# A score bank for the second FFN group of a double step, normalizations deferred by length, and casts moved ahead of their PE transposes

## The chip, the cores and the metric

The kernel runs on one core of a Trainium2 chip. The metric is the device time of one execution in microseconds (us). The time before is 454.0 us, the median of two runs (453.2 to 454.79).

## The reference, cut to what matters

```python
B, H, S, Nb, D = (8, 8, 576, 16, 64)
k_all = concatenate([beacon_k, k]);  v_all = concatenate([beacon_v, v])
scores = (q @ k_all.T) / sqrt(D)         # causal over k; the 16 beacon keys are always seen
a = exp(scores - max);  a /= a.sum(-1) + 1e-9
x = (a @ v_all), transposed to (4608, 512)           # 4608 = 8 * 576 rows
out = (relu(x @ w_gate) * (x @ w_val)) @ w_out       # 512 -> 1536 -> 512
```

All matmuls take bf16 (so says every record of one in the traces) and write tiles of FP32; the PE transposes write bf16 ones. The kernel takes no maximum away before the exponential; it checks at the end that the row sums were in a safe range, and has a general path for when they were not.

## The kernel before

The attention of one pair of heads is cut into four steps, by chunks of queries: step 0 fills a chunk of 240 columns, steps 1 and 2 together one of 256, step 3 one of 80. Two steps make a double step of the loop. In a double step PE makes two score groups, two groups of the FFN (an "up" group is four matmuls for g and four for u, a "down" group twelve), and the value products of the double step before. ScalarE (ACT) takes exponentials and relu, VectorE (DVE) takes reciprocals and products, GpSimd (Pool) masks and casts.

A bank is here what a tile of 512 FP32 columns takes in PSUM. The pool of scores has two tiles of two banks, the pool of value products two of one bank, and the FFN pool two of one bank: 2x2 + 2 + 2, eight banks in all.

```python
    s_ps = ...tile_pool(name="s_ps", bufs=2, space=PSUM)    # tiles [P, 2, 512] FP32: two banks each
    o_ps = ...tile_pool(name="o_ps", bufs=2, space=PSUM)    # [P, 2, 256]: product and row sums
    f_ps = ...tile_pool(name="f_ps", bufs=2, space=PSUM)    # [P, 512]: g, u, down
    ...
    def normalize(pr, i):                     # only if i ends its chunk
        nc.vector.reciprocal(r, o[:, 1, :cn])
        nc.vector.tensor_mul(xT[:, pr.p, t0:t0 + cn], o[:, 0, :cn], r)

        def up(self, nf, c0, c1):
            g = f_ps.tile([P, M_TILE], FP32, name="f")
            ... 4 matmuls into g
            nc.scalar.activation(gs[:, :n], g[:, :n], AF.Relu)
            u = f_ps.tile([P, M_TILE], FP32, name="f")
            ... 4 matmuls into u
            nc.vector.tensor_mul(self.h[:, nf, c0:c1], gs[:, :n], u[:, :n])

        def turn_pair(b, x, p, copy, ps_pool):
            h = half.tile([P, 4, P], BF16, name="half")
            copy(h..., wide[b, x, p]...)                        # cast to bf16
            ps = ps_pool.tile([P, 4, P], BF16, ...)
            for r in range(4):
                nc.tensor.transpose(ps[:, r], h[:, r], ident)   # PE, at once after its cast
            copy(dst..., ps...)

        for s0 in range(0, len(work) + STRIDE, STRIDE):         # STRIDE = 2: a double step
            ...
            for s in now:
                ... qk, and the first softmax
            for s in now:
                ... later actions, the second softmax
                if queue:
                    queue.pop(0)()                              # one FFN group
                if waiting:
                    normalize(*waiting.pop())
            for s in range(s0 - STRIDE, s0):
                ... av(pairs[b, p], i)
                waiting.append((pairs[b, p], i))
                if s == s0 - STRIDE or not queue:
                    normalize(*waiting.pop())
        ...
        for j, g in enumerate(queue):                           # FFN groups left after the attention
            if j == 2:
                ok = rows_in_range()
            if j == 8:
                in_range = count(ok)
            g()
```

So the first normalization of a double step is done at once, and the second waits until the first FFN group of the next double step has been issued. Of the first batches (0 and 1), a pair's steps run in the order 0, (1, 2), 3. From batch 2 on, a batch does (1, 2) for its four pairs and then (0, 3) for its four pairs.

Of the kernel before, what the change touches and what calls it, by code (L numbers as in the profile page):

```python
# [10 lines left out]
FP32 = mybir.dt.float32  # L11
BF16 = mybir.dt.bfloat16
# [134 lines left out]
def kernel(  # L147
# [12 lines left out]
    nc = tc.nc  # L160
    B, H, S, D = q.shape
    Nb = beacon_k.shape[2]
    P = 128
    d_model = H * D
    n_tokens = B * S
    d_ff = moe_w_gate.shape[1]
    KM, NF = d_model // P, d_ff // P
    NP = H // 2
# [3 lines left out]
    M_TILE = 512  # L172
# [4 lines left out]
    ident = const.tile([P, P], BF16, name="ident")  # L177
# [10 lines left out]
    main = ctx.enter_context(ExitStack())  # L188
    kvq = main.enter_context(tc.tile_pool(name="kvq", bufs=2))
    stage = main.enter_context(tc.tile_pool(name="stage", bufs=11))  # L190
    half = main.enter_context(tc.tile_pool(name="half", bufs=6))
    psb = main.enter_context(tc.tile_pool(name="psb", bufs=4))
    nrm = main.enter_context(tc.tile_pool(name="nrm", bufs=2))
    fsb = main.enter_context(tc.tile_pool(name="fsb", bufs=2))
# [1 line left out]
    s_ps = main.enter_context(tc.tile_pool(name="s_ps", bufs=2, space=bass.MemoryType.PSUM))  # L196
    o_ps = main.enter_context(tc.tile_pool(name="o_ps", bufs=2, space=bass.MemoryType.PSUM))
    f_ps = main.enter_context(tc.tile_pool(name="f_ps", bufs=2, space=bass.MemoryType.PSUM))
# [101 lines left out]
    def normalize(pr, i):  # L300
        ci = CHUNK_OF_STEP[i]
        cq0, cn, _, last = CHUNKS[ci]
        if i != last:
            return
        o, batch = pr.o[ci], pr.batch
        r = batch.r[:, pr.p, cq0:cq0 + cn]
        nc.vector.reciprocal(r, o[:, 1, :cn])  # L307
        t0 = batch.b * S + cq0
        nc.vector.tensor_mul(xT[:, pr.p, t0:t0 + cn], o[:, 0, :cn], r)  # L309
        batch.chunks += 1  # L310
        if batch.chunks == NP * len(CHUNKS):
            nc.sync.dma_start(
                rsum[2 * batch.b:2 * batch.b + 2],
                batch.r.rearrange("(a x) p s -> a x (p s)", a=2)[:, 0])


    class Ffn:
# [1 line left out]
        def __init__(self, m0):  # L319
            self.m0, self.h = m0, None  # L320

        def up(self, nf, c0, c1):
            n = c1 - c0
            if self.h is None:
                self.h = fsb.tile([P, NF, M_TILE], BF16, name="hT")
            x = xT[:, :, self.m0 + c0:self.m0 + c1]
            g = f_ps.tile([P, M_TILE], FP32, name="f")
            for ki in range(KM):
                nc.tensor.matmul(g[:, :n], wg[:, ki, nf * P:(nf + 1) * P], x[:, ki],  # L329
                                 start=(ki == 0), stop=(ki == KM - 1))  # L330
            gs = fsb.tile([P, M_TILE], FP32, name="g")
            nc.scalar.activation(gs[:, :n], g[:, :n], AF.Relu)  # L332
            u = f_ps.tile([P, M_TILE], FP32, name="f")
            for ki in range(KM):
                nc.tensor.matmul(u[:, :n], wv[:, ki, nf * P:(nf + 1) * P], x[:, ki],  # L335
                                 start=(ki == 0), stop=(ki == KM - 1))
            nc.vector.tensor_mul(self.h[:, nf, c0:c1], gs[:, :n], u[:, :n])  # L337
# [9 lines left out]
            nc.sync.dma_start(out[m:m + P, :], ob)  # L347

        def groups(self, c0, c1, d0, d1):
            return ([lambda nf=nf: self.up(nf, c0, c1) for nf in range(NF)]  # L350
                    + [lambda ms=ms: self.down(ms) for ms in range(d0, d1)])

    def rows_in_range():

# [23 lines left out]
    with tc.manual_schedule():  # L378
# [3 lines left out]
        rest = S - WIDE  # L382
        wide = {}
        vec, act, pool = nc.vector.tensor_copy, nc.scalar.copy, nc.gpsimd.tensor_copy
# [13 lines left out]
                nc.sync.dma_start(t[p0:p0 + a.shape[1]].rearrange("p (h d) -> p h d", d=D),  # L398
                                  a.rearrange("h p d -> p h d"))

        def turn_pair(b, x, p, copy, ps_pool):
            h = half.tile([P, 4, P], BF16, name="half")
            copy(h.rearrange("x r (h d) -> x h r d", d=D),  # L403
                 wide[b, x, p].rearrange("x (h r d) -> x h r d", h=2, d=D))
            ps = ps_pool.tile([P, 4, P], BF16, name="f" if ps_pool is f_ps else "s")
            for r in range(4):
                nc.tensor.transpose(ps[:, r], h[:, r], ident)  # L407
            dst, off = (batches[b].kT, Nb) if x == "k" else (batches[b].qT, 0)
            copy(dst[:, p, off:off + WIDE].rearrange("x (p r) -> x p r", r=4),  # L409
                 ps.rearrange("x r p -> x p r"))  # L410

        def turn_tail(b, x, copy, ps_pool):
            n = rest + (Nb if x == "k" else 0)
            h = half.tile([P, d_model], BF16, name="half")
            copy(h[:n], wide[b, x][:n])  # L415
            ps = ps_pool.tile([P, NP, P], BF16, name="f" if ps_pool is f_ps else "s")
            for p in range(NP):
                nc.tensor.transpose(ps[:, p, :n], h[:n, p * P:(p + 1) * P], ident[:n, :n])
            if x == "k":
                copy(batches[b].kT[:, :, Nb + WIDE:Stot], ps[:, :, :rest])  # L420
                copy(batches[b].kT[:, :, :Nb], ps[:, :, rest:n])
            else:
                copy(batches[b].qT[:, :, WIDE:], ps[:, :, :rest])
# [18 lines left out]
        ahead, later = {}, {}  # L442

        def at(step, action, when=later):
            when.setdefault(step, []).append(action)

        for p in range(NP):
            at(p, lambda p=p: turn_pair(0, "k", p, vec, f_ps), ahead)
            at(p, lambda p=p: turn_pair(0, "q", p, act, f_ps), ahead)
            if p == 0:  # L450
                at(p, lambda: turn_tail(0, "k", vec, f_ps), ahead)
        at(4, lambda: turn_tail(0, "q", vec, f_ps), ahead)
        for t, step in enumerate((0, 1, 2, 4, 4)):
            at(step, lambda t=t: batches[0].cast("v", t, pool))
        for w, step in zip(weights, (0, 0, 1, 1, 2, 2, 4, 4, 4)):
# [4 lines left out]
        def fetch_wide(b, load, turn):  # L460
            at(load, lambda: batches.append(Batch(b)))
            units = [lambda p=p, x=x: load_pair(b, x, p) for p in range(NP) for x in "kq"]
            units[2:2] = [lambda: load_tail(b, "k")]
            units[5:5] = [lambda: batches[b].load("v", 0), lambda: batches[b].load("v", 1)]
            units += [lambda: load_tail(b, "q")]
            units += [lambda t=t: batches[b].load("v", t) for t in range(2, NKT)]
            for j, u in enumerate(units):
                at(load + j * 2 // 3, u)
            for p in range(NP):
                at(turn + p, lambda p=p: turn_pair(b, "k", p, vec, s_ps))  # L470
                at(turn + p, lambda p=p: turn_pair(b, "q", p, act, s_ps))
            at(turn + 1, lambda: turn_tail(b, "k", vec, s_ps))
            at(turn + 4, lambda: turn_tail(b, "q", vec, s_ps))
            for t in range(NKT):
                at(turn + t, lambda t=t: batches[b].cast("v", t, pool))

# [14 lines left out]
        for b in range(B):  # L491
# [7 lines left out]
                ready[len(work)] = (b + 1) * S  # L499
            if b == 0:  # L500
                work += [None] * GAP
        fetch_wide(1, 4, 17)
        for b in range(2, B):
            fetch(b, 16 * (b - 1) + GAP)

# [3 lines left out]
        queue, have, pairs, waiting = [], 0, {}, []  # L509
        STRIDE = 2  # L510
# [7 lines left out]
        for s0 in range(0, len(work) + STRIDE, STRIDE):  # L518
            have = ready.get(s0 - STRIDE, have)
            while spans and spans[0][1] <= have:  # L520
                add_ffn()
            now = [s for s in range(s0, s0 + STRIDE) if s < len(work)]
            for s in now:
                for action in ahead.get(s, []):
                    action()
                if work[s]:
                    b, p, i = work[s]
                    qk(pairs.setdefault((b, p), Pair(batches[b], p)), i)
                    if s == s0 or s < 4:
                        softmax(pairs[b, p], i)  # L530
            for s in now:
                for action in later.pop(s, []):
                    action()
                if work[s] and not (s == s0 or s < 4):
                    b, p, i = work[s]
                    softmax(pairs[b, p], i)
                if queue:
                    queue.pop(0)()
                if waiting:
                    normalize(*waiting.pop())  # L540
            for s in range(s0 - STRIDE, s0):
                if 0 <= s < len(work) and work[s]:
                    b, p, i = work[s]
                    av(pairs[b, p], i)

                    waiting.append((pairs[b, p], i))
                    if s == s0 - STRIDE or not queue:
                        normalize(*waiting.pop())
        for w in waiting:
            normalize(*w)  # L550
        while spans:
# [1 line left out]
        for j, g in enumerate(queue):  # L553
            if j == 2:
                ok = rows_in_range()
            if j == 8:
                in_range = count(ok)
            g()
    main.close()
    with tc.If(in_range < 2 * B):  # L560
        general_path(tc, q, k, v, beacon_k, beacon_v, out, ident, wg, wv, wo)
# [30 lines left out]
```

## Time and profile before

| what | before |
|---|---|
| time | 454.0 us |
| span of the profiled execution, granted clock | 447.7 us, 0.989 |
| PE busy | 401.4 us, 90% |
| period of one batch in the steady part (start of a block of down groups to the next) | 44.1 us |
| first scores of batch 1 | 69.65 us |

The first fence is from the page of the kernel before: its busy line, and two lines of the span in 40 slices (busy tenths of PE, and the granted clock in tenths).

```profile
PE 401.4 (90%) x3681; PEld 218.2 (49%) x3681; DVE 249.5 (56%) x355; ACT 200.5 (45%) x313; POOL 123.3 (28%) x283
...
PE   2479579898988999999999999999999788999995
...
PEclk9999989999999999999999999999999989999998
```

PE is busy 90% of the span, but that number says little here. The records of PE overlap: the record of the u group at 241.93 us lasts 1.03 us, and that of the next g begins 0.86 us after its start. What can be trusted is the distance from the first start of a group to the first start of the next. A group of four 512-column matmuls that has nothing in its way takes 0.86 us, and one of 48 such matmuls takes 10.36 us, 215.8 ns each.

The next fence is the wait list of the kernel before: engine, tile and line that waited, what for, us in total, number of times, longest.

```profile
PE o L294 <- DVE xT L309: 12.0, 11, 2.3
...
PE f L418 <- DVE half L415: 5.4, 2, 3.9
...
PE s L407 <- DVE half L403: 4.0, 3, 1.7
```

L294 is the value product, L309 the product that ends a normalization, L403 and L415 are casts, L407 and L418 are PE transposes. The timeline shows single places (start, duration, engine, line, operation, out<-in, idle time before and what ended it):

```profile
50.53 0.62 PE L407 MATMUL s<-ident,half 128*128 128x128 bf16 x8 [1.75 <-DVE half L403]
...
54.13 0.62 PE L407 MATMUL s<-ident,half 128*128 128x128 bf16 x8 [1.31 <-DVE half L403]
...
242.79 1.03 PE L329 MATMUL f<-xT,wg 128*128 128x512 bf16 x4
...
243.06 0.69 DVE L337 TENSOR_TENSOR hT<-g,f 128x512 bf16<-128x512 f32 x1 [6.83 <-PE f L335]
...
243.80 1.02 PE L335 MATMUL f<-xT,wv 128*128 128x512 bf16 x4
...
253.74 1.75 DVE L307 RECIPROCAL r<-o 128x256 f32<-128x256 f32 x1
...
255.53 0.42 DVE L309 TENSOR_TENSOR xT<-o,r 128x256 bf16<-128x256 f32 x1
...
256.00 0.23 PE L294 MATMUL o<-e,v 128*64 128x80 bf16 x2 [0.67 <-DVE xT L309]
```

Three losses are in it. At 50.53 and 54.13 us PE waits for a cast that was issued just in front of the transposes that read it. At 242.79 the second g of a double step takes until 243.80, 1.01 us rather than 0.86: the u behind it needs the bank of the first u, and DVE's product reads that bank until 243.06 + 0.69 = 243.75. The wait list doesn't show this loss, because the record of g, which lasts until 242.79 + 1.03 = 243.82, counts as busy until then. And at 256.00 a value product waits for a bank that a deferred 256-column reciprocal (1.75 us) and product still hold.

### The profile page before, as it was taken

The numbers are of one execution on the slowest core, as the hardware profiler recorded it, in microseconds if no ns is written. First come the engines' busy times: TensorE is split into PE (matmuls) and PEld (weight loads), VectorE is DVE, ScalarE is ACT, GpSimd is POOL, SyncE is SP. The second block draws the span as 40 slices with busy tenths as digits, with TensorE's granted clock in tenths as the row PEclk, the third lists the DMA queues.
The fourth block names the chain that finished last, engine by engine and source line by source line (L and its number), as shares of the span: only waits on it lengthen the run. The fifth ranks groups of instructions, "written<-read, shape, count | busy, mean of one in ns | idle before, by whom it ended". The sixth has DMA issues, their size and how long they took to land.

```text
span 447.7 us, 9258 instructions
## 1 busy us (share of the span) xinstructions
PE 401.4 (90%) x3681; PEld 218.2 (49%) x3681; DVE 249.5 (56%) x355; ACT 200.5 (45%) x313; POOL 123.3 (28%) x283
## 2 busy tenths in 40 slices
PE   2479579898988999999999999999999788999995
PEld 1257446466567445554555455545554343444442
DVE  3457745747579368537853785378637863331320
ACT  3446336356455545454544554446455312322321
POOL 1842204342454444224422442243112100000000
PEclk9999989999999999999999999999999989999998
DMA  9999945885995783379447863790110002002002
GB/s 221 226 211 227 186 102 101 163 152 107 156 202 125 179 184 78 85 197 171 92 91 192 157 116 83 160 180 15 49 48 2 1 4 92 2 0 95 0 16 85
DMA packets 143522, 51.00 MB, mean 114 GB/s; under 512 B 129120, under 2 KB 138848, under 8 KB 143456
## 3 DMA queue, kind: packets, MB, share of 16 engines
q1 hardware_dynamic: 137152, 45.09, 48.6%
q0 software_dynamic: 5776, 4.72, 6.6%
q8 instruction: 31, 0.51, 0.5%
q10 hardware_dynamic: 544, 0.52, 0.3%
q14 instruction: 19, 0.16, 0.1%
HBM read 38.27 MB, written 9.44 MB: 107 GB/s over the span
## 4 chain that ended last, share of the span: by engine, by line
PE 79%; DVE 12%; issue 4%; ACT 2%; DMA 1%; SPq 0%; ACTq 0%; DVEq 0%
PE f L342 21%; PE f L335 20%; PE f L329 19%; PE o L294 11%; DVE r L307 7%; PE s L263 6%; DVE hT L337 3%; DVE xT L309 1%; DMA raw<-in_beacon_k_dram 1%; ACT g L332 1%; ACT half L403 1%; PE s L407 0%; PE f L407 0%; ACT qT L409 0%; DVE half L415 0%
## 5 line engine op out<-in xcount | busy, mean ns | idle before, releaser
L337 DVE TENSOR_TENSOR hT<-g,f 128x512 bf16<-128x512 f32 (+4 forms) x132 | 77.5, 587 | 141.5 <-PE f L335 118.4
L271 ACT ACTIVATE e<-s 128x736 bf16<-128x736 f32 (+3 forms) x128 | 110.5, 864 | 95.4 <-PE s L263 94.9
L307 DVE RECIPROCAL r<-o 128x240 f32<-128x240 f32 (+2 forms) x96 | 129.7, 1351 | 21.9 <-PE o L294 21.9
L329 PE MATMUL f<-xT,wg 128*128 128x512 bf16 (+4 forms) x528 | 117.0, 344 | 6.1 <-ACT g L332 2.7
L274 POOL TENSOR_SCALAR_AFFINE_SELECT e<-e 128x256 bf16<-128x256 bf16 (+2 forms) x160 | 58.8, 387 | 221.0 <-ACT e L271 211.2
L335 PE MATMUL f<-xT,wv 128*128 128x512 bf16 (+4 forms) x528 | 114.9, 340 | 0.6
L332 ACT ACTIVATE g<-f 128x512 f32<-128x512 f32 (+4 forms) x132 | 68.6, 520 | 67.3 <-PE f L329 65.5
L342 PE MATMUL f<-wo,hT 128*128 128x512 bf16 x432 | 97.3, 383 | 0.3 <-ACT g L332 0.3
L335 PEld LDWEIGHTS <-wv 128*128 128x128 bf16 x528 | 51.0, 97 | 55.5 <-issue 18.7
L329 PEld LDWEIGHTS <-wg 128*128 128x128 bf16 x528 | 47.0, 98 | 48.2 <-issue 11.9
L294 PE MATMUL o<-e,v 128*64 128x80 bf16 (+4 forms) x704 | 58.5, 239 | 12.0 <-DVE xT L309 12.0
L342 PEld LDWEIGHTS <-hT 128*128 128x128 bf16 x432 | 41.7, 99 | 51.1 <-issue 4.0
L294 PE MATMUL o<-e,ones 128*64 128x80 bf16 (+4 forms) x704 | 53.4, 233 | 0.0
L294 PEld LDWEIGHTS <-v 128*64 128x64 bf16 (+1 forms) x704 | 35.3, 112 | 36.0 <-issue 26.3
L345 ACT COPY ob<-f 128x512 f32<-128x512 f32 x36 | 21.1, 585 | 68.1 <-PE f L342 62.7
L263 PE MATMUL s<-qT,kT 64*128 64x80 bf16 (+3 forms) x704 | 36.1, 233 | 2.5 <-ACT qT L409 2.0
L309 DVE TENSOR_TENSOR xT<-o,r 128x240 bf16<-128x240 f32 (+2 forms) x96 | 34.3, 358 | 3.3
L294 PEld LDWEIGHTS <-ones 128*64 128x64 bf16 (+1 forms) x704 | 35.4, 113 | 0.1
L239 POOL CAST half<-raw 128x512 bf16<-128x512 f32 (+2 forms) x60 | 35.0, 611 | 0.0
L263 PEld LDWEIGHTS <-kT 64*128 64x128 bf16 x704 | 22.4, 96 | 9.1 <-issue 3.1
L239 POOL CAST v<-raw 128x512 bf16<-128x512 f32 (+1 forms) x40 | 24.4, 616 | 8.0 <-DMA raw<-in_v_dram 8.0
L407 PEld LDWEIGHTS <-half 128*128 128x128 bf16 x64 | 4.6, 114 | 15.1 <-DVE half L403 9.7
(36 smaller groups left out, 50.1 us busy)
## 6 DMA issues: line engine op xcount, KB each, us to landing
out_dram<-ob SPq DMA_DIRECT2D x36, 256.0 KB, 2.2
raw<-in_q_dram SPq DMA_DIRECT2D x30, 256.0 KB, 4.2
raw<-in_k_dram SPq DMA_DIRECT2D x26, 256.0 KB, 5.0
raw<-in_v_dram SPq DMA_DIRECT2D x24, 256.0 KB, 3.8
raw<-in_v_dram SPq DMA_DIRECT2D x8, 224.0 KB, 4.1
wg<-in_moe_w_gate_dram POOLq DMA_DIRECT2D x4, 384.0 KB, 12.0
wv<-in_moe_w_val_dram POOLq DMA_DIRECT2D x4, 384.0 KB, 14.4
wo<-in_moe_w_out_dram POOLq DMA_DIRECT2D x1, 1536.0 KB, 28.3
```

The lines of the kernel that those rows point to most:

```text
L239: copy(dst, self.raw[x, t][:n])
L263: nc.tensor.matmul(s[:, a, c:c + n], pr.batch.kT[rows, pr.p, kt * P:(kt + 1) * P], pr.batch.qT[rows, pr.p, q0:q0 + n], start=True, stop=True)
L271: nc.scalar.activation(e[:, :, :n], pr.s[i][:, :, :n], AF.Exp, scale=scale)
L274: nc.gpsimd.affine_select(out=e[:, :, c:c + m], in_=e[:, :, c:c + m], pattern=[[0, 2], [1, m]], compare_op=ALU.is_ge, fill=0.0, base=base, ...
L294: nc.tensor.matmul(o[rows, part, q0 - cq0:q0 - cq0 + n], w, e[:kr, a, c:c + n], start=(i == first and j == 0 and part == 0), stop=(i == la ...
L307: nc.vector.reciprocal(r, o[:, 1, :cn])
L309: nc.vector.tensor_mul(xT[:, pr.p, t0:t0 + cn], o[:, 0, :cn], r)
L329: nc.tensor.matmul(g[:, :n], wg[:, ki, nf * P:(nf + 1) * P], x[:, ki], start=(ki == 0), stop=(ki == KM - 1))
L332: nc.scalar.activation(gs[:, :n], g[:, :n], AF.Relu)
L335: nc.tensor.matmul(u[:, :n], wv[:, ki, nf * P:(nf + 1) * P], x[:, ki], start=(ki == 0), stop=(ki == KM - 1))
L337: nc.vector.tensor_mul(self.h[:, nf, c0:c1], gs[:, :n], u[:, :n])
L342: nc.tensor.matmul(o, self.h[:, nf, ms * P:(ms + 1) * P], wo[:, nf, :], start=(nf == 0), stop=(nf == NF - 1))
```

## The change

Its intent is to take these three waits from PE. It has three parts, and no arithmetic is added.

*Bank.* The second FFN up group of a double step puts its u in a score tile; so do all groups after the attention.

```diff
-        def up(self, nf, c0, c1):
+        def up(self, nf, c0, c1, u_pool=None):
...
-            u = f_ps.tile([P, M_TILE], FP32, name="f")
+            if u_pool is None:
+                u = f_ps.tile([P, M_TILE], FP32, name="f")
+            else:
+                u = u_pool.tile([P, 2, 512], FP32, name="s")[:, 0]
...
-                    queue.pop(0)()
+                    queue.pop(0)(None if s == s0 else s_ps)
...
-            g()
+            g(s_ps)
```

*Norm.* A normalization that ends the 256-column chunk (i is 2) is no longer deferred; only those of 240 and 80 columns are.

```diff
-                    waiting.append((pairs[b, p], i))
-                    if s == s0 - STRIDE or not queue:
-                        normalize(*waiting.pop())
+                    if s == s0 - STRIDE or i == 2 or not queue:
+                        normalize(pairs[b, p], i)
+                    else:
+                        waiting.append((pairs[b, p], i))
```

*Casts.* Casting and turning become two functions, and the cast runs one double step ahead of its PE transposes. The pool of cast tiles gets two more buffers. In the first batch, Pool casts q pairs 1 to 3 and the q tail.

```diff
-    half = main.enter_context(tc.tile_pool(name="half", bufs=6))
+    half = main.enter_context(tc.tile_pool(name="half", bufs=8))
...
+        def first_casts(p):
+            cast_pair(0, "k", p, vec)
+            cast_pair(0, "q", p, pool if p else act)
...
+        at(3, lambda: cast_tail(0, "q", pool), ahead)
+        at(4, lambda: turn_tail(0, "q", act, f_ps), ahead)
...
-                at(turn + p, lambda p=p: turn_pair(b, "k", p, vec, s_ps))
-                at(turn + p, lambda p=p: turn_pair(b, "q", p, act, s_ps))
-            at(turn + 1, lambda: turn_tail(b, "k", vec, s_ps))
-            at(turn + 4, lambda: turn_tail(b, "q", vec, s_ps))
+                for x, c in (("k", vec), ("q", act)):
+                    at(turn + p, lambda x=x, p=p, c=c: cast_pair(b, x, p, c))
+                    at(turn + p + 2, lambda x=x, p=p, c=c: turn_pair(b, x, p, c, s_ps), ahead)
+            at(turn + 1, lambda: cast_tail(b, "k", vec))
+            at(turn + 3, lambda: turn_tail(b, "k", vec, s_ps), ahead)
+            at(turn + 4, lambda: cast_tail(b, "q", vec))
+            at(turn + 6, lambda: turn_tail(b, "q", vec, s_ps), ahead)
...
-        fetch_wide(1, 4, 17)
+        fetch_wide(1, 4, 16)
```

More of the change, by code (lines that the diff above doesn't have):

```diff
@@ L349, in groups @@
         def groups(self, c0, c1, d0, d1):
-            return ([lambda nf=nf: self.up(nf, c0, c1) for nf in range(NF)]
-                    + [lambda ms=ms: self.down(ms) for ms in range(d0, d1)])
+            return ([lambda pool=None, nf=nf: self.up(nf, c0, c1, pool) for nf in range(NF)]
+                    + [lambda pool=None, ms=ms: self.down(ms) for ms in range(d0, d1)])
     def rows_in_range():
@@ L399, in load_tail, with cast_pair, cast_tail, bank @@
                                   a.rearrange("h p d -> p h d"))
-        def turn_pair(b, x, p, copy, ps_pool):
-            h = half.tile([P, 4, P], BF16, name="half")
+        turned = {}
+        def cast_pair(b, x, p, copy):
+            h = turned[b, x, p] = half.tile([P, 4, P], BF16, name="half")
             copy(h.rearrange("x r (h d) -> x h r d", d=D),
                  wide[b, x, p].rearrange("x (h r d) -> x h r d", h=2, d=D))
-            ps = ps_pool.tile([P, 4, P], BF16, name="f" if ps_pool is f_ps else "s")
+        def cast_tail(b, x, copy):
+            n = rest + (Nb if x == "k" else 0)
+            h = turned[b, x] = half.tile([P, d_model], BF16, name="half")
+            copy(h[:n], wide[b, x][:n])
+        def bank(ps_pool):
+            return ps_pool.tile([P, 4, P], BF16, name="f" if ps_pool is f_ps else "s")
+        def turn_pair(b, x, p, copy, ps_pool):
+            ps = bank(ps_pool)
             for r in range(4):
-                nc.tensor.transpose(ps[:, r], h[:, r], ident)
+                nc.tensor.transpose(ps[:, r], turned[b, x, p][:, r], ident)
             dst, off = (batches[b].kT, Nb) if x == "k" else (batches[b].qT, 0)
@@ L413, in turn_tail @@
             n = rest + (Nb if x == "k" else 0)
-            h = half.tile([P, d_model], BF16, name="half")
-            copy(h[:n], wide[b, x][:n])
-            ps = ps_pool.tile([P, NP, P], BF16, name="f" if ps_pool is f_ps else "s")
+            ps = bank(ps_pool)
             for p in range(NP):
-                nc.tensor.transpose(ps[:, p, :n], h[:n, p * P:(p + 1) * P], ident[:n, :n])
+                nc.tensor.transpose(ps[:, p, :n], turned[b, x][:n, p * P:(p + 1) * P],
+                                    ident[:n, :n])
             if x == "k":
@@ L445, in at, with first_turns @@
             when.setdefault(step, []).append(action)
-        for p in range(NP):
-            at(p, lambda p=p: turn_pair(0, "k", p, vec, f_ps), ahead)
-            at(p, lambda p=p: turn_pair(0, "q", p, act, f_ps), ahead)
-            if p == 0:
-                at(p, lambda: turn_tail(0, "k", vec, f_ps), ahead)
-        at(4, lambda: turn_tail(0, "q", vec, f_ps), ahead)
+        def first_casts(p):
+            cast_pair(0, "k", p, vec)
+            cast_pair(0, "q", p, pool if p else act)
+        def first_turns(p):
+            turn_pair(0, "k", p, vec, f_ps)
+            turn_pair(0, "q", p, act, f_ps)
+        first_casts(0)
+        cast_tail(0, "k", vec)
+        first_turns(0)
+        turn_tail(0, "k", vec, f_ps)
+        first_casts(1)
+        for p in range(1, NP):
+            at(p, lambda p=p: first_turns(p), ahead)
+            if p + 1 < NP:
+                at(p, lambda p=p: first_casts(p + 1), ahead)
+        at(3, lambda: cast_tail(0, "q", pool), ahead)
+        at(4, lambda: turn_tail(0, "q", act, f_ps), ahead)
         for t, step in enumerate((0, 1, 2, 4, 4)):
```

## The prediction

> **What bounds the kernel.** The page's busy table has PE at 401 of 447.7 us (90%), DVE 249, ACT 201; the chain of waits is 79% PE, 12% DVE. But 90% busy hides waits: [...] So I count starts. A group of four 512-column matmuls takes 0.86 us from its first start to the next group's, if nothing is in its way. Four losses:
>
> 1. *u waits for the previous u's product.* f has two banks, so the second u of a double step starts only when DVE has multiplied the first (timeline: product ends 243.75, u starts 243.80). The g group ahead then takes 1.01 us. Between 147 and 354 us there are 29 such groups (4.2 us), after 360 us 22 (3.3 us).
> 2. *The deferred 256-column normalization* (reciprocal 1.75 us, product 0.42) holds an o bank too long: the wait list has "PE o <- DVE xT" 12.0 us, 11 times. At each change from steps (1,2) to (0,3) the value product takes 1.66 instead of 0.80 us (5 times, 4.3 us); similar stalls at 47 us (1.07), 103 us (1.16) and 129 us (1.28). That at 79 us (1.2) is of a 240-column one, which stays deferred; two at 354-360 us stay too.
> 3. *Casts in front of the second batch's PE transposes*: between 50 and 66 us PE waits about 6.8 us for half tiles.
> 4. *Start*: PE waits 3.9 us (19.5-23.5) for the q tail's cast behind two reciprocals.
>
> **What the change does.** No arithmetic is added. (1) goes: u takes a score bank, free since an exponential that ended a microsecond earlier; the score matmul that next needs this bank waits for a product that ends before it. 4.2 + 3.3 us, plus 0.7 among the small groups before 147 us. (2): 4.3 + 1.1 + 1.2 + 1.3, about 7.5 us. (3): about half comes back: four or five transposes in one burst over two score banks still wait for copies (0.69 DVE, 0.58 ACT), some 1.6 and 1.0 us; and the first output group, at 55.9 us, needs w_out, whose transfer landed at 52.75 us, so at most 3 us can be won before it. I take 4 us. (4): little. The four 240-column normalizations (2.06 us each) end before the first FFN group can; and Pool casts q pair 3 only after issuing four weight transfers (0.8 us each), so the first value products start later (20 instead of 18.1 us), but DVE then runs through. I take 0.7 us.
>
> Sum: 8.2 + 7.5 + 4.7 = about 20 us, nearly all on the critical path, as PE is it.
>
> **Predicted: 434 us, range 429 to 441** (8 in 10). Faster by over 2%: 0.96; same 0.035; slower 0.005.
>
> **What would show it.** Steady up groups all at 0.86-0.88 us; batch period 42.4 instead of 44.1 us; "PE o <- DVE xT" about 5 us; no "PE s <- DVE half"; a wait for w_out (PE f <- DMA wo) near 50-53 us; first FFN group still near 29 us; final tile 32.3 instead of 34.1 us.
>
> **What would make it wrong.** Score matmuls waiting for u's product (PE s <- DVE hT); DVE short of time at 134-145 us, where it is 94% busy (windows), so that waits only change name; w_out landing later; Pool, with three more casts of 0.61 us, delaying masks.

## The result, and the profile after

The changed kernel took 429.71 us (median of 2 runs, 429.07 to 430.35), against 454.0 before. A ratio here is the mean time of one kernel's runs over the mean of the other's in the same rounds, so it is not quite the ratio of the medians. It is 0.9465 (95% interval 0.9372 to 0.9558). A later job ran the same changed kernel again: 429.48 us (6 runs) against 452.24 (11 runs), ratio 0.9501 (0.9474 to 0.9528). The prediction was 434 us, range 429 to 441.

| what | before | after |
|---|---|---|
| span of the profiled execution, granted clock | 447.7 us, 0.989 | 427.4 us, 0.996 |
| PE busy | 401.4 us, 90% | 386.7 us, 90% |
| period of one batch in the steady part | 44.1 us | 42.4 us |
| first value product | 18.10 us | 19.85 us |
| first scores of batch 1 | 69.65 us | 63.53 us |
| last value stage, from its first start to the next group's | 6.62 us | 7.03 us |
| one of the last tiles, free of the wait for the row count | 32.68 us | 31.08 us |

The page of the changed kernel, the same three lines:

```profile
PE 386.7 (90%) x3631; PEld 219.5 (51%) x3681; DVE 252.3 (59%) x353; ACT 199.7 (47%) x311; POOL 125.4 (29%) x287
...
PE   2469888999998999999999999999999698999995
...
PEclk9999999999999999999999999999999989999999
```

Its wait list:

```profile
PE o L294 <- DVE xT L309: 7.4, 6, 2.3
...
PE f L422 <- POOL half L408: 3.7, 1, 3.7
...
PE f L345 <- DMA wo<-in_moe_w_out_dram: 0.8, 1, 0.8
...
PE s L263 <- DVE hT L340: 0.7, 2, 0.3
```

The waits of transposes in score banks for DVE's casts are gone from the list. A wait for w_out is new. The wait of the first batch's tail (3.9 us) has turned into one of a pair for Pool's cast (3.7 us). The wait that was feared, of score matmuls (L263) for the product of u (L340), is 0.7 us in all. The timeline of the changed kernel (L338 is now u, L340 its product, L422 and L431 the transposes, L345 the down group):

```profile
18.14 0.61 PE L422 MATMUL f<-ident,half 128*128 128x128 bf16 x4 [3.75 <-POOL half L408]
...
29.84 1.01 PE L329 MATMUL f<-xT,wg 128*128 128x240 bf16 x4
...
30.64 1.01 PE L338 MATMUL s<-xT,wv 128*128 128x240 bf16 x4
...
49.20 0.88 PE L422 MATMUL s<-ident,half 128*128 128x128 bf16 x8
...
53.03 2.75 PE L345 MATMUL f<-wo,hT 128*128 128x512 bf16 x11 [0.81 <-DMA wo<-in_moe_w_out_dram]
...
240.23 0.42 DVE L309 TENSOR_TENSOR xT<-o,r 128x256 bf16<-128x256 f32 x1
...
240.51 1.03 PE L329 MATMUL f<-xT,wg 128*128 128x512 bf16 x4
...
240.78 0.69 DVE L340 TENSOR_TENSOR hT<-g,f 128x512 bf16<-128x512 f32 x1
...
241.37 1.03 PE L338 MATMUL s<-xT,wv 128*128 128x512 bf16 x3
...
242.51 0.69 DVE L340 TENSOR_TENSOR hT<-g,s 128x512 bf16<-128x512 f32 x1 [1.04 <-PE s L338]
...
339.77 0.29 PE L294 MATMUL o<-e,v 128*64 128x240 bf16 x2 [2.15 <-DVE xT L309]
```

The second g starts at 240.51 and its u at 241.37, 0.86 us later, although DVE's product of the first u ends only at 240.78 + 0.69 = 241.47. That is the bank part at work. The transposes at 49.20 start without a wait. At 339.77, after the last scores, a value product still waits 2.15 us for a normalization.

Where the 20.3 us of span went can be read from four landmarks of the two traces, and set beside the terms of the prediction for the same stretches:

| stretch | before | after | gain | predicted |
|---|---|---|---|---|
| start to the value products near 45.5 us | 45.69 | 45.47 | 0.2 | 0.7 |
| from there to the first scores of batch 1 | 23.96 | 18.06 | 5.9 | 5.1 (casts 4, norm 1.1) |
| from there to the last value stage | 284.19 | 273.22 | 11.0 | 11.3 (bank 4.9, norm 6.4) |
| from there to the end | 93.86 | 90.65 | 3.2 | 3.3 (bank) |

### The profile page after: what moved, and what is told of

It is laid out like the page before. It is cut to its first block, busy times and chain, and to the rows that moved or that the text cites. A ratio compares the mean times of both kernels' runs of the same rounds, so it can differ in the third digit from the quotient of the medians.

```text
span 427.4 us, 9193 instructions
## 1 busy us (share of the span) xinstructions
PE 386.7 (90%) x3631; PEld 219.5 (51%) x3681; DVE 252.3 (59%) x353; ACT 199.7 (47%) x311; POOL 125.4 (29%) x287
## 4 chain that ended last, share of the span: by engine, by line
PE 78%; DMA 8%; issue 4%; DVE 3%; POOL 2%; ACT 2%; SPq 1%; ACTq 0%; DVEq 0%; POOLq 0%
PE f L345 22%; PE f L329 20%; PE s L338 13%; PE o L294 11%; PE f L338 6%; DMA wo<-in_moe_w_out_dram 6%; PE s L263 6%; DVE r L307 2%; ACT g L332 1%; DVE hT L340 1%; DMA raw<-in_q_dram 1%; DMA raw<-in_k_dram 1%; POOL v L239 1%; POOL wg L249 1%; POOL wv L249 0%
## 5 line engine op out<-in xcount | busy, mean ns | idle before, releaser
L329 PE MATMUL f<-xT,wg 128*128 128x512 bf16 (+4 forms) x508 | 114.1, 343 | 8.5 <-ACT g L332 3.0
L345 PE MATMUL f<-wo,hT 128*128 128x512 bf16 x416 | 94.1, 379 | 2.6 <-issue 1.0
L340 DVE TENSOR_TENSOR hT<-g,s 128x512 bf16<-128x512 f32 (+4 forms) x79 | 47.9, 606 | 71.3 <-PE s L338 66.9
L338 PEld LDWEIGHTS <-wv 128*128 128x128 bf16 x528 | 51.9, 99 | 44.8 <-issue 2.6
L338 PE MATMUL s<-xT,wv 128*128 128x512 bf16 (+4 forms) x311 | 71.3, 349 | 0.4
L345 PEld LDWEIGHTS <-hT 128*128 128x128 bf16 x432 | 41.4, 98 | 51.0 <-issue 3.1
L294 PE MATMUL o<-e,ones 128*64 128x80 bf16 (+4 forms) x704 | 52.6, 233 | 0.0
L338 PE MATMUL f<-xT,wv 128*128 128x512 bf16 (+4 forms) x203 | 44.1, 331 | 0.5
L263 PE MATMUL s<-qT,kT 64*128 64x80 bf16 (+3 forms) x704 | 36.4, 233 | 3.2 <-ACT qT L424 2.0
L340 DVE TENSOR_TENSOR hT<-g,f 128x512 bf16<-128x512 f32 (+4 forms) x53 | 29.9, 564 | 15.5 <-PE f L338 11.7
L309 DVE TENSOR_TENSOR xT<-o,r 128x240 bf16<-128x240 f32 (+2 forms) x96 | 34.4, 358 | 3.3
L263 PEld LDWEIGHTS <-kT 64*128 64x128 bf16 x704 | 22.4, 96 | 10.1 <-issue 3.1
## 6 DMA issues: line engine op xcount, KB each, us to landing
wg<-in_moe_w_gate_dram POOLq DMA_DIRECT2D x4, 384.0 KB, 11.3
```

The costliest lines, as they stand in the source:

```text
L263: nc.tensor.matmul(s[:, a, c:c + n], pr.batch.kT[rows, pr.p, kt * P:(kt + 1) * P], pr.batch.qT[rows, pr.p, q0:q0 + n], start=True, stop=True)
L294: nc.tensor.matmul(o[rows, part, q0 - cq0:q0 - cq0 + n], w, e[:kr, a, c:c + n], start=(i == first and j == 0 and part == 0), stop=(i == la ...
L329: nc.tensor.matmul(g[:, :n], wg[:, ki, nf * P:(nf + 1) * P], x[:, ki], start=(ki == 0), stop=(ki == KM - 1))
L338: nc.tensor.matmul(u[:, :n], wv[:, ki, nf * P:(nf + 1) * P], x[:, ki], start=(ki == 0), stop=(ki == KM - 1))
L345: nc.tensor.matmul(o, self.h[:, nf, ms * P:(ms + 1) * P], wo[:, nf, :], start=(nf == 0), stop=(nf == NF - 1))
```

## The experiments

The questions were three. Do the parts of the change act alone, or do they need each other? Is the start bound by PE and the casts, or by the transfers of the weights? And is what the changed kernel still waits for worth anything? Twelve kernels ran, in three jobs; each job also ran the kernel before on the same chip. The 95% interval of every ratio below leaves out 1. All outputs are right.

### The bank alone

The edit is the bank part of the change on top of the kernel before, as in the first diff above.

> The kernel before with the score bank for u alone (second up group of a double step, and all up groups after the attention); normalizations and casts as before. Theory A, the parts add up: the 1.01 us groups become 0.86, 29 x 0.145 us in the steady part and 22 x 0.148 us at the end, so 454 - 8 = about 446 us, and no PE s <- DVE hT waits. Theory B, the score bank needs the other normalization rule: in the double steps where a 256-column normalization (2.17 us) is still deferred between the two products, the second product ends about 3.5 us after the first u ended, but the second score group wants its bank 2.0 to 3.0 us after it; so 0.6 to 0.9 us of a new wait PE s <- DVE hT in each of about 16 such double steps (5 to 9 us together), only the last tiles (after 360 us) gain 3.3 us: 454 to 460 us, no faster than before.

Measured: 460.07 us (4 runs) against 452.42 (7 runs), ratio 1.0184 (1.0146 to 1.0223). The bank alone makes the kernel slower by about 8 us, a little more than the 0 to 6 us that theory B allowed. Its wait list:

```profile
PE o L294 <- DVE xT L309: 13.0, 11, 2.3
PE s L263 <- DVE hT L340: 11.9, 18, 0.8
```

and its timeline at one of those 18 places:

```profile
211.88 1.03 PE L338 MATMUL s<-xT,wv 128*128 128x512 bf16 x4
211.89 1.75 DVE L307 RECIPROCAL r<-o 128x256 f32<-128x256 f32 x1
...
214.01 0.68 DVE L340 TENSOR_TENSOR hT<-g,s 128x512 bf16<-128x512 f32 x1
...
214.74 0.35 PE L263 MATMUL s<-qT,kT 64*128 64x80 bf16 x10 [0.69 <-DVE hT L340]
```

The second u is in a score tile and is done soon after 212.8, but DVE can't multiply it before 214.01: the deferred 256-column reciprocal stands in front of it in DVE's order. The next score group needs that tile and waits until 214.74. So the bank moved the wait for DVE from u to the scores, and made it longer. The gain that was predicted for the bank was also there: the second g of a double step took 0.86 us. But the period of a batch was 45.1 us rather than 44.1.

What follows: the bank gives nothing by itself. It lets PE run ahead of DVE, and that pays only if DVE is not held up by a long deferred normalization.

### The normalization alone

The edit is the second diff above on top of the kernel before.

> The kernel before with only the normalization rule changed (256 columns at once, only short ones and 240-column ones of the second slot deferred). If the o bank held too long was the cause: the 1.66 us value groups become 0.80 (5 times), the stalls at 47, 103 and 129 us go, PE o <- DVE xT falls from 12.0 to about 5 us, and the time falls by about 7.5 us to 446.5 (443 to 449). The g groups of 1.01 us stay. If the waits only change name (DVE short of time): less than 3 us.

Measured: 448.98 us (4 runs) against 452.42, ratio 0.9926 (0.989 to 0.9961). That is a gain of 3.4 us, where the prediction's term was 7.5. The steady part did what it should: the period fell from 44.1 to 43.27 us and "PE o <- DVE xT" to 5.5 us in 3 waits. Some was given back in the small double steps of the first batches, as this timeline shows:

```profile
99.72 1.76 DVE L307 RECIPROCAL r<-o 128x256 f32<-128x256 f32 x1 [0.35 <-PE o L294]
...
101.28 0.68 PE L329 MATMUL f<-xT,wg 128*128 128x304 bf16 x4
...
101.86 0.46 DVE L337 TENSOR_TENSOR hT<-g,f 128x304 bf16<-128x304 f32 x1
...
102.37 0.68 PE L335 MATMUL f<-xT,wv 128*128 128x304 bf16 x4 [0.41 <-DVE hT L337]
```

The undeferred reciprocal now starts before the first u is done, so DVE's product of that u comes late (101.86), and the second u, with only two FFN banks, waits for it. From 101.28 to 102.37 the second g takes 1.09 us; in the kernel before it took 0.51 to 0.64 at this width. Over the stretch from the first scores of batch 1 (72.29 us) to the down groups at 185.38, the gain is 0.85 us of profile, where the kernel before had stalls of about 2.4 us (103 and 129 us) and one change of steps (0.86) to win. Before 46 us the profile loses 3.2 us more; a stretch of half clock lies there, from 31.0 to 34.4 us (mean clock from 30 to 35 us: 0.66), that the kernel before did not have (1.00), so how much of this the edit caused stays open.

### Bank and normalization together

The edit is both of these on top of the kernel before; the casts stay as they were.

> Score bank and normalization rule together, casts as before. 454 - 8.2 - 7.5 = about 438 us (435 to 441), no PE s <- DVE hT waits, up groups at 0.86-0.88 us. Under theory B this is more than the sum of the two alone by 8 us or more; under theory A it is their sum.

Measured: 437.56 us (4 runs) against 452.42, ratio 0.9659 (0.9593 to 0.9725). The product of the two ratios alone is 1.0184 x 0.9926 = 1.0109, so together they are 4.5% better than they would be if they only added up. In its profile the period is 42.4 us, "PE s <- DVE hT" is 0.7 us in 2 waits, and "PE o <- DVE xT" 5.6 us in 4. The waits of transposes for DVE's casts are there as in the kernel before (4.0 us, 3 times).

What follows: each part removes the wait that the other one creates. Without the bank, the undeferred reciprocal delays the u product, and so the next u; with the bank nothing waits for that product at once. Without the norm part, the bank's u product stands behind the deferred reciprocal; with it, the reciprocal is done by then: in the changed kernel's timeline above the 256-column normalization ends at 240.23 + 0.42 = 240.65, before DVE's first product starts at 240.78.

### The casts alone

The edit takes the bank and norm parts out of the changed kernel.

> The kernel before with only the casts moved (first batch and second batch, half pool 8, turn step 16). Predicted share: 4 us at 46-70 us and 0.7 us at the start, 449 us (447 to 451). PE s <- DVE half goes; the first score group of the second batch comes about 4 us sooner than at 69.65 us; PE waits for w_out or its transposes' copies instead. If only the start mattered: under 1.5 us.

Measured: 444.54 us (4 runs) against 452.42, ratio 0.9829 (0.9798 to 0.986), a gain of 7.9 us, more than the 3 to 7 us that were expected. In the profiles the gain is smaller: the span is 442.6 against 447.7 us, and the first scores of batch 1 come at 64.65 rather than 69.65 us, 5.0 us sooner. The period is 44.1 us, as in the kernel before. The difference between the 7.9 us and the 5.1 of the spans goes with the clock: this kernel's runs have a granted clock of 0.990 to 0.993, those of the kernel before in the same job a median of 0.981, while the profiled run of the kernel before had 0.989.

The product of the ratios of the casts and of bank with norm is 0.9829 x 0.9659 = 0.9494, and the changed kernel, run again in the third job, had 0.9501. So these two halves of the change do add up.

### The start: one more cast moved, and the first down group later

The changed kernel's first value product waits for Pool's cast of q pair 3, which stands behind four weight transfers that Pool issues and two casts of v (fence above, 18.14 us). The first edit has DVE cast it:

```diff
-            cast_pair(0, "q", p, pool if p else act)
+            cast_pair(0, "q", p, (act, pool, pool, vec)[p])
```

> The changed kernel with the cast of the first batch's q pair 3 on DVE instead of behind four weight issues on Pool. PE's 3.75 us wait for that cast (14.4-18.1 us) goes, the first value products start at about 16 instead of 19.85 us, the first FFN group near 25-26 instead of 29 us. Theory D, the start is bound by transfers: the last part of w_val lands at 42.7 us and w_out at 53.0 us whatever PE does, so the first output group stays at 53.0 us, PE waits there about 3 us instead of 0.8, and the time stays at 429.7 within 0.7 us. Rival, the cast is on the critical path: 3.5 us faster, 426.

Measured: 432.38 us (4 runs), 0.9562 of the kernel before in its job (451.33 us, 7 runs). It is not faster than the changed kernel, and 2.2 us slower than the next edit (430.17 us) in the same job. The first value product came at 15.73 us, 4.1 sooner, and the first u at 25.09 rather than 29.04. The time was then lost again, since the transfers of the weights did not come sooner (w_out landed at 53.26 us, against 53.0 in the changed kernel). Its wait list and two stretches (us from and to, length, busy us and count of PE, PEld, DVE, ACT and POOL, then granted clock, DMA share and GB/s) show it:

```profile
PE f L345 <- DMA wo<-in_moe_w_out_dram: 3.5, 1, 3.5
...
PE s L338 <- DMA wv<-in_moe_w_val_dram: 0.7, 1, 0.7
```

```profile
49.20:52.60 3.40, 0.30 (x4) 0.20 (x4) 2.15 (x7) 1.08 (x2) 0.00 (x0) 1.00 1.23 226
52.60:56.10 3.50, 2.80 (x7) 1.01 (x7) 0.00 (x0) 0.00 (x0) 1.62 (x3) 0.51 0.45 91
```

The first down group waits 3.5 us for w_out, PE is nearly idle from 49.2 to 52.6, and in the next 3.5 us the granted clock is half (0.51): its twelve matmuls take 3.93 us, and 2.59 in the changed kernel. The half clock is a cost that nobody had expected here.

The second edit leaves that down group for later, after the up groups of the second chunk:

```diff
-            queue.extend(f.groups(c0, c1, c0 // P, c1 // P))
+            d0, d1 = {0: (0, 0), 240: (0, 4)}.get(t0, (c0 // P, c1 // P))
+            queue.extend(f.groups(c0, c1, d0, d1))
```

> The changed kernel with the first output group moved behind the next span's up groups, so that w_out is not needed before about 75 us. Theory D alone: only the 0.8 us wait for w_out goes, 429 us. If w_out held up more than the wait list says, 2 us or more.

Measured: 430.17 us (4 runs), ratio 0.9503, which is the changed kernel's time within the noise. Then both edits together:

> Both. Theory D: now the 3.75 us of the cast count, as far as the last part of w_val (lands 42.7 us, first used at 44.96 us in the changed kernel) lets them, so 2.2 + 0.8 = about 3 us faster than the changed kernel, 426.7 us, more than the two alone together (about 1 us). First score group of the second batch near 60.5 instead of 63.5 us. If the cast counts by itself, f1 and f2 add up.

Measured: 427.18 us (4 runs, 425.67 to 427.86), ratio 0.9449 (0.9398 to 0.95). The first scores of batch 1 come at 58.95 rather than 63.53 us, 4.6 sooner. In its job it is 5.2 us under the first edit and 3.0 us under the second, and no runs overlap. The changed kernel itself was not in this job; against its 429.5 to 429.7 us of the others the gain is about 2 us, but the intervals of the two ratios (0.9398 to 0.95, and 0.9474 to 0.9528) overlap. So there are two limits in a row at the start, a late cast and a late w_out. The first edit alone only moves PE's wait from the cast to w_out; the second alone leaves the wait for the cast (3.7 us) and gains nothing. Part of the gain of both may be clock: near 53 us the profiles of the single edits have a stretch of half clock each, and this one has none (PEclk in the sixth of the 40 slices: 8, 8 and 9 tenths).

### The last value stage

In the last double step no scores are left, and the loop pops an FFN group only where there are. So two value stages stand next to each other with normalizations between them and nothing for PE to do (fence above, 339.77 us). The edit puts two FFN groups there, and the waiting normalization in its usual place behind the first:

```diff
+            if not now:
+                for _ in range(2):
+                    queue.pop(0)(s_ps)
+                    if waiting:
+                        normalize(*waiting.pop())
             for s in range(s0 - STRIDE, s0):
```

> The changed kernel with two FFN groups taken in the last pass of the loop too, before its value products, so that PE has 3.5 us of work while DVE normalizes. The two waits of 2.15 and 2.29 us and the half-rate clock after them (3.4 us of records, 1.7 us of loss at most) go: 5 to 6 us faster, about 424 us. If the waits only move to the next value products: under 2 us.

Measured: 423.38 us (4 runs, 422.82 to 424.8), ratio 0.937 (0.9317 to 0.9423), 6.3 us under the changed kernel. Its timeline in that place:

```profile
337.14 1.65 DVE L307 RECIPROCAL r<-o 128x240 f32<-128x240 f32 x1
...
337.16 1.04 PE L329 MATMUL f<-xT,wg 128*128 128x512 bf16 x4
...
338.82 0.41 DVE L309 TENSOR_TENSOR xT<-o,r 128x240 bf16<-128x240 f32 x1
```

PE works while DVE normalizes, both value stages take 0.80 us, and there is no stretch of half clock after them (PEclk is 9 tenths in all slices but the last), whereas the kernel before and the changed kernel both have one of 3.4 us there (granted clock 0.50 from 359.0 and from 342.2 us).

### A version that beats both

The changed kernel once more, for its time in the same job as the best version:

> The changed kernel itself once more, beside the next three on one chip and against the kernel before with more rounds: 430 us (428 to 432), ratio 0.945 to 0.957.

Measured: 429.48 us (6 runs), as told above.

The best version has the three edits (cast, down group, last stage) and one more: the count of rows in range is read into a register at group 14 of the tail rather than at group 8, where PE waited 1.3 us for it.

```diff
             if j == 8:
-                in_range = count(ok)
+                cnt = count(ok)
+            if j == 14:
+                in_range = load_count(cnt)
```

> The changed kernel with the q pair 3 cast on DVE, the first output group later (f3), two groups in the last pass (f4), and the loads of the row count into the engines' registers six groups later than the count itself (PE waited 1.3 us for it at 361.8 us of the changed kernel). If the gains add up: 2.5 + 6.3 + 1.3 = 10 us under the changed kernel, about 420 us.

Measured: 418.44 us (6 runs, 418.24 to 419.59) against 452.24 (11 runs), ratio 0.9256 (0.9233 to 0.9279). It is 7.4% under the kernel before, and 11.0 us, 2.6%, under the changed kernel. Its span is 416.5 us, with PE busy 93% of it; the wait for the count is gone from its wait list.

### Both halves of the second group in one score tile

A score tile has two banks, and u uses one of them. In the best version the second g of a small double step still waits for the relu of the first g, whose FFN bank it takes: with 304 columns the first u takes 0.68 to 0.87 us to the start of that g. If the second g used the other bank of the score tile, it would need no FFN bank at all. On top of the best version:

```diff
-            g = f_ps.tile([P, M_TILE], FP32, name="f")
+            if u_pool is None:
+                g = f_ps.tile([P, M_TILE], FP32, name="f")
+            else:
+                gu = u_pool.tile([P, 2, 512], FP32, name="s")
+                g = gu[:, 1]
...
-                u = u_pool.tile([P, 2, 512], FP32, name="s")[:, 0]
+                u = gu[:, 0]
```

> g1_best, and the second g of a double step (and all after the attention) in the other, unused half of the score tile that its u takes. In the changed kernel this g waits for the rectifier of the first g, which stands behind an exponential on ACT: the u group before it takes 0.81-0.95 instead of 0.45-0.52 us in some 14 small double steps between 29 and 136 us. In the score tile it waits only for the exponential: some 0.3 us each, 3 to 4.5 us less than g1_best, about 416 us. If the wait was for the exponential itself: no gain.

Measured: 474.75 us (6 runs), ratio 1.0496 (1.0471 to 1.0522). This is a miss: it is 56 us slower than the best version. Its wait list and timeline (L342 is u here, L336 the relu, L333 g):

```profile
PE s L342 <- ACT g L336: 52.4, 79, 0.9
```

```profile
300.51 1.03 PE L333 MATMUL s<-xT,wg 128*128 128x512 bf16 x3
...
301.57 0.60 ACT L336 ACTIVATE g<-s 128x512 f32<-128x512 f32 x1 [0.40 <-PE s L333]
...
302.22 1.02 PE L342 MATMUL s<-xT,wv 128*128 128x512 bf16 x4 [0.69 <-ACT g L336]
```

The wait that the edit aimed at did go: with 304 columns the first u takes 0.52 to 0.55 us. But now u waits for the relu that reads g, in another bank of the same tile, 79 times. The waits are in the built program: by the trace, 79 u groups in score tiles wait for ACT's semaphore, against one in the best version. We infer that dependencies were tracked by the tile and not by its halves. The last run changes on top of this which normalizations are deferred. Now all are done at once except those of step 3:

```diff
-                    if s == s0 - STRIDE or i == 2 or not queue:
+                    if s == s0 - STRIDE or i != 3 or not queue:
```

> g2_pair with the 240-column normalizations at once too (only those of 80 columns deferred). Only two double steps of the second batch have such a deferred one beside FFN groups; the value product that waits 1.15 us near 73 us of the changed kernel should wait about 0.5 us: 0 to 1 us less than g2_pair.

Measured: 475.4 us (6 runs), ratio 1.0503. Under the new wait, the order of normalizations makes no difference, so this run says nothing of what it would do without that wait. Left open: g of the second group in a score tile and its u in an FFN bank, two tiles, which would not have this dependency if that inference holds.

## Why the prediction was right

The time, 429.71 us, fell in the range of 429 to 441, near its lower end, and the reasons were mostly the right ones.

1. *Bank and norm in the steady part: right.* The predicted period was 42.4 us and the measured one 42.4. The second g fell from 1.01 to 0.86 us everywhere, the value product after a change of steps from 1.66 to 0.80 us. From the first scores of batch 1 to the last value stage the gain was 11.0 us, and the terms of the prediction for that stretch add up to 11.3. The tile near the end was predicted to go from 34.1 to 32.3 us. The 34.1 included the wait for the row count, and that tile measured 32.65; a tile without it went from 32.68 to 31.08. The difference is 1.6 us, 11 times 0.15, which is the term as it was costed.

2. *But the sum treated bank and norm as independent, and they are not.* The prediction wrote 8.2 us for the one and 7.5 for the other. Alone they gave -7.7 us (460.07 against 452.42) and +3.4. It named the risk itself ("Score matmuls waiting for u's product (PE s <- DVE hT)"); the bank alone shows that wait at 11.9 us, and it is the norm part that keeps it at 0.7. The prediction came out right because both were in the change.

3. *Casts: about right.* The stretch from 45.5 us to the first scores of batch 1 became 5.9 us shorter; 5.1 were predicted for it. Of the 5.9, 1.3 is the norm's (the value stage at its start took 0.85 us instead of 2.11), and 1.4 is a difference of clock: in the profile of the kernel before, the first down group fell in a stretch of half clock (0.51 from 55.2 to 58.7 us) and took 3.96 us, in that of the changed kernel 2.59. What is left is 3.2 us, and 4 were predicted. The prediction also said what caps it, w_out, and the wait for it came at 53.03, 0.8 us long. With the casts alone, which reach the first down group at 54.32 us and find w_out there, the stretch from the same value stage to the first scores of batch 1 was 18.0 us; that is 6.0 shorter, or 4.6 without the clock.

4. *Start: little, as predicted.* The first value product came later (19.85 instead of 18.10; "20" was predicted), for the reason that was given, Pool's cast behind the weights that it issues. The u of the first FFN group came 0.6 us sooner (29.04 against 29.65 us). What the prediction did not see is how slowly PE starts. The trace's record of the clock begins, at full clock, at 31.55 us in the changed kernel and at 27.94 us in the kernel before (the 9s of PEclk in front of that stand for no record, so the clock of that time is not shown). In the changed kernel groups take about twice as long until then: 0.80 us from 29.84 to 30.64, where the same group takes 0.42 at 32.95. On the three groups from 29.04 us that costs about 1 us, an estimate, which is enough for the start to have gained 0.2 us where 0.7 were predicted. The begin of the record goes with the cast of q pair 3: in the five traces in which PE waits for Pool to do it, the record begins at 31.6 to 33.3 us, and in the other nine at 23.3 to 28.8; the first edit of the start, which moves this cast alone, has 28.75.

5. *"PE o <- DVE xT about 5 us": it was 7.4.* Two new waits at the start, 0.51 and 1.27 us at 22.9 and 25.0 us, were not foreseen, and the one at 79 us stayed, as was said.

6. *Where the 4.3 us between 434 and 429.71 came from.* The predicted "about 20" was right for the profiles: 447.7 to 427.4 is 20.3. The step that failed was to subtract it from 454.0. The profiled run of the kernel before took 449.39 us at a clock of 0.989; its other runs took 449.48 to 454.79 us, at clocks of 0.971 to 0.992 where the clock is on record. So the 20 us was read from one of its fastest runs and taken from its median. The changed kernel's timed runs have 0.986 to 0.996, so that its median gains what the profile doesn't show. (These means need care: the 0.989 of the kernel before counts 3.3 us of half clock from 444.4 us on, when PE had done its last matmul at 442.3.) The two-run median of 454.0 is itself 1.6 to 2.7 us above those of the three later jobs (451.33 to 452.42). A loss by clock is about as large as the difference: a stretch of half clock lasted 3.4 us in the two traces (clock 0.50 to 0.51) and costs at most half of it, 1.7, by estimate. These two stretches are of the profiled run of the kernel before (columns as above):

```profile
51.80:55.20 3.40, 1.64 (x50) 1.24 (x48) 2.18 (x6) 1.17 (x3) 0.61 (x1) 1.00 0.84 158
55.20:58.70 3.50, 3.06 (x11) 1.30 (x12) 1.91 (x7) 0.17 (x1) 1.30 (x2) 0.51 0.00 0
```

PE is busy for 1.64 of 3.4 us while it waits for casts, and the clock is then half in the next 3.5 us. That fewer waits of PE make such stretches rarer fits the runs: the casts alone raise the clock from 0.981 to 0.990 and more, and filling the last stage removed the stretch behind it (0.994 to 0.998, where the changed kernel's runs have 0.986 to 0.996). It was not tested by itself, and the clock of the same kernel differs from run to run (0.996 and 0.989 in the two profiled runs of the changed kernel), so this much stays open.

## What to carry to other kernels

When PE is busy 90% of the time, measure the distance between the starts of its groups: a wait for a bank can hide inside the busy time of the group ahead (here 0.15 us, 1.01 instead of 0.86). Giving a product a bank of its own can move the wait to whoever needs that bank next (here 11.9 us, in 18 waits of the score matmuls), so look at what stands in front of its reader on the other engine, and expect two parts of a change to need each other. Before subtracting a gain read from one profile, check where the time and the clock of that profiled run lie among the runs of the same kernel.

## What the traces showed of the hardware

- 48 pairs of a weight load and a 512-column matmul in a row took 10.36 us to the start of the next group in the kernel before (from 365.04 us), 215.8 ns each. From first start to last end they took 10.52 us there, and as much in the changed kernel (from 411.63 us), whose trace has 47 of the 48.
- The clock fell to half (0.51) after 3.4 us in which PE was busy 1.64 us and its longest gap was 1.31 us (before, 51.80 to 55.20). What makes it fall was not tested. The half-clock stretches that end within the span lasted 3.4 us in the kernel before and in the changed kernel; with the normalization alone, a mean clock of 0.66 from 355 to 365 us makes it about 6.8 us there, an estimate (0.34 x 10 / 0.5).
- The reciprocal took 1.75 us for 128x256, 1.65 for 128x240 and 0.65 for 128x80 out of PSUM tiles, so about 6.2 ns for each further column ((1.75 - 0.65) / 176); the product that follows took 0.42, 0.41 and 0.24, about 1 ns. The interplay of bank and norm rests on that difference.
- Each transfer of w_gate and w_val held Pool for 0.75 to 0.90 us and that of w_out for 1.05, and a cast behind four of them came 3.7 us too late for PE.
